# Attention sums kept transposed on four column tiles, with the softmax denominators sent through DRAM

## The chip, the cores and the metric

One Trainium2 chip, one of its cores. The metric is the device time of one execution in microseconds, the median of several runs. The time before is 291.59 us (three runs, 291.12 to 291.71).

## What is computed

A gated mix of two branches over one sequence of 2048 tokens with 512 features, all in bf16. Branch A is attention with a compressive memory: 32 heads of 16 features, four segments of 512 tokens, causal softmax attention inside a segment and a linear memory that is read before each segment's keys and values are added to it. Branch B is a gated MLP with 1792 hidden features.

```python
# branch A, for each segment s of 4 (L = 512 tokens), H = 32 heads, Dh = 16
logits = einsum('bhqd,bhkd->bhqk', qs, ks) * Dh**-0.5 + causal_mask
a_dot  = einsum('bhqk,bhkd->bhqd', softmax(logits), vs)
pq     = phi(qs)                        # t + 1 if t > 0 else exp(t)
a_mem  = (pq @ M) / (pq @ z + 1e-6)
o      = sigmoid(beta) * a_mem + (1 - sigmoid(beta)) * a_dot
M, z   = M + phi(ks).T @ vs, z + phi(ks).sum(over l)
a      = o @ wo
# branch B
b      = (gelu(x @ w_gate) * (x @ w_up)) @ w_down
# mix
g      = sigmoid((x * gate_w).sum(-1))
out    = g * a + (1 - g) * b
```

## The kernel before

**Chunks and groups.** Heads go in chunks `c` of eight (128 features), four chunks to a segment, 16 in all. The eight heads of a chunk are four pairs; `p` = 0 or 1 names the even or the odd head of each pair, and a chunk has two sides, p = 0 and p = 1. For each chunk, five groups A to E make the lower triangle of the logits: `group_qk` (L514) puts four heads on four row tiles of TensorE (32 rows each), one exp of 128x2048 on ScalarE turns the logits tile `lg` (four PSUM banks, one buffer) into `pT` (keys on partitions, queries along the free axis; five buffers), and GpSimd's `affine_select` (L543) zeroes what lies above the diagonal. There are 80 groups.

**Sums of values.** `pv` (L547) takes 128x128 blocks of `pT` as weights and 17 columns of V (16 features and a one) as the moving side, and so makes sums and denominators in rows of queries: 40 matmuls for a side. `finish` (L557) divides: a reciprocal of the denominators, a multiplication by one minus the head's gate, and a multiplication from PSUM into `o2`. The memory's share is `tm` (L507, VectorE, out of `mem_num`) and is added to `o2` (L804); a transposing DMA (L570) then makes `oT` with features on partitions, which `u_out` (L412) multiplies by `wo`. The memory's denominators come from `u_den` (L472).

**Other work, and the order.** K, Q, V, gate, up, down and out projections, the memory update `u_M`, and the masks are units in nine streams. A planner written into the kernel keeps modelled times of TensorE and ScalarE (`passed`, `act`), emits one group's logits when it believes that the exp before it has ended, and fills the time between with units: `fill_to` (L654) takes the unit with the smallest wanted group number plus a weight for VectorE's backlog. `clock` counts groups, `later(n, f)` puts a step n groups on, and `after` (L785) holds what follows each group. The result is one fixed order of instructions on each engine; engines run in order and meet by semaphores. Three PSUM banks (`gen`) serve all units, one serves `od`. All DMAs are issued by SyncE (SP).

**Buffers.** `xT` holds all four segments of x. `G` holds the gate activations, three buffers of 14 blocks of 512, so that gates of segment 3 wait for `down` of segment 0. `osb`, the output rows, has three buffers.

A second path (`general`) recomputes everything with row maxima if a bound on the logits fails; with these inputs it isn't run.

The lines that decide the order around the groups:

```python
goal = ready_at + max(0.0, slack) / (n + 1)
fill_to(t_pe[0] + 0.5 * (goal - t_pe[0]))
for f in pending:
    f()
pending.clear()
fill_to(goal)
t_pe[0] = max(t_pe[0], ready_at)
pending.append(lambda a=(s, c, g, mine, oT, state): after(*a))
```

Of the kernel before, what the change touches and what calls it, by code (L numbers as in the profile page):

```python
# [13 lines left out]
P = 128  # L14
D = 512
# [8 lines left out]
NG = 3  # L24
# [8 lines left out]
QK_T = 0.41  # L33
TURN = 0.15
# [10 lines left out]
def kernel(  # L45
# [29 lines left out]

    def const(shape, dtype, name):
        return cpool.tile(shape, dtype, name=name, tag=name)

    xT = const([P, FC, S], BF, "xT")
# [13 lines left out]
    og = const([P, H], F32, "og")  # L93
    Macc = const([P, NC8, 8, 17], F32, "Macc")
    Mn = [const([P, NC8, 128], BF, f"Mn{i}") for i in range(2)]
    Mz = [const([P, NC8, 8], BF, f"Mz{i}") for i in range(2)]
    rdm = [const([P, KT, H], F32, f"rdm{i}") for i in range(2)]
# [3 lines left out]
    G = [const([P, HS, L], BF, f"G{i}") for i in range(NG)]  # L101
# [4 lines left out]
    V = [const([P, KT, H, 18], BF, f"V{i}") for i in range(2)]  # L106
# [7 lines left out]

    def gen(name):
        return pgen.tile([P, 512], F32, name=name, tag="gen")

    def load_inputs():
        def cols(dst, src):
            nc.sync.dma_start(dst[:, :, :], src.rearrange("(fc p) n -> p fc n", p=P))  # L120

        def x_seg(s):
            nc.sync.dma_start_transpose(xT[:, :, s * L:(s + 1) * L], x2[s * L:(s + 1) * L, :])
# [11 lines left out]
        x_seg(3)  # L135
# [3 lines left out]

    x0 = G[1][:, 0:KT, :]  # L140
    zero = G[1][:, KT, :]

# [23 lines left out]
    def setup_consts():  # L166
# [9 lines left out]
        for i in range(2):  # L176
            nc.gpsimd.memset(V[i][:, :, :, 16:17], 1.0)
        nc.gpsimd.memset(Macc[:, :, :, :], 0.0)

    def setup_beta():  # L180
# [5 lines left out]
                                op0=ALU.mult, op1=ALU.add)  # L186

# [6 lines left out]
    def u_absmax_x(s):  # L194
        def f():
            for fc in range(FC):
                def g(fc=fc):
                    absmax(4 * (s - 1) + fc, xT[:, fc:fc + 1, s * L:(s + 1) * L])
                    passed(0.0, 0.6)
                later(1 + fc, g)  # L200
# [37 lines left out]
    def u_q(s, c):  # L238
        def f():
            T = gen("qT")  # L240
            for fc in range(FC):
                nc.tensor.matmul(T[:, :], lhsT=wq[:, fc, c * P:(c + 1) * P],  # L242
                                 rhs=xT[:, fc, s * L:(s + 1) * L],
# [9 lines left out]
    due = {}  # L253

    def later(n, f):
        due.setdefault(clock[0] + n, []).append(f)

    general_now = [False]
# [34 lines left out]
    def u_k(s, c):  # L293
        def f():
            T = gen("kT")
            for fc in range(FC):
                nc.tensor.matmul(T[:, :], lhsT=wk[:, fc, c * P:(c + 1) * P],  # L297
                                 rhs=xT[:, fc, s * L:(s + 1) * L],
# [16 lines left out]
    def u_v(s, kt):  # L315
        def f():
            T = gen("vT")
            for fc in range(FC):
                nc.tensor.matmul(T[:, :], lhsT=xT[:, fc, s * L + kt * P:s * L + (kt + 1) * P],  # L319
                                 rhs=wv[:, fc, :], start=(fc == 0), stop=(fc == FC - 1))  # L320
                if fc < FC - 1:
                    yield MM512
            nc.vector.tensor_copy(V[s % 2][:, kt, :, 0:16],
                                  T[:, :].rearrange("p (h d) -> p h d", h=H))
# [3 lines left out]
    def u_gate_logits(s):  # L328
        def f():
            T = gen("zT")  # L330
            for qt in range(KT):
                t = s * KT + qt
                for fc in range(FC):
                    nc.tensor.matmul(T[:, qt:qt + 1], lhsT=xT[:, fc, t * P:(t + 1) * P],
# [3 lines left out]
            if s < NSEG - 1:  # L338
                return 0.44
            g2 = gct[:, :, :].rearrange("p s q -> p (s q)")  # L340
            o2 = omg[:, :, :].rearrange("p s q -> p (s q)")
# [5 lines left out]
            def f_gate():  # L347
# [4 lines left out]
                done["gate"] = 1  # L352
# [6 lines left out]
    def u_gate(s, hs, direct):  # L359
        def f():  # L360
            T = gen("gT")
            for fc in range(FC):
                nc.tensor.matmul(T[:, :], lhsT=wga[:, fc, hs * P:(hs + 1) * P],  # L363
                                 rhs=xT[:, fc, s * L:(s + 1) * L],
# [3 lines left out]
            if direct:  # L368
                nc.scalar.activation(G[s % NG][:, hs, :], T[:, :], AF.Gelu_apprx_tanh)  # L369
            else:  # L370
                nc.vector.tensor_copy(G[s % NG][:, hs, :], T[:, :])  # L371
# [3 lines left out]
    def gelu(s):  # L375
        for h0 in range(0, HS, 7):
            g = G[s % NG][:, h0:h0 + 7, :]
            nc.scalar.activation(g, g, AF.Gelu_apprx_tanh)  # L378

    def u_up(s, hs):  # L380
        def f():
            T = gen("uT")
            for fc in range(FC):
                nc.tensor.matmul(T[:, :], lhsT=wup[:, fc, hs * P:(hs + 1) * P],  # L384
                                 rhs=xT[:, fc, s * L:(s + 1) * L],
# [3 lines left out]
            g = G[s % NG][:, hs, :]  # L389
# [6 lines left out]
    def u_down(s, qt):  # L396
        def f():
            T = gen("dT")
            for hs in range(HS):
                nc.tensor.matmul(T[:, :], lhsT=G[s % NG][:, hs, qt * P:(qt + 1) * P],  # L400
# [11 lines left out]
    def u_out(s, qt):  # L412
        def f():
# [7 lines left out]
            if s == NSEG - 1:  # L421

                osb = G[(s + 1) % NG][:, qt, :]
            else:
                osb = wk2.tile([P, D], BF, name="osb", tag="osb", bufs=3)[:, :]
# [8 lines left out]
    def u_M(s, half):  # L434
        def f():
            T = gen("MT")
            Tv = T[:, 0:272].rearrange("p (c h e) -> p c h e", c=2, h=8)
            for cc in range(2):
                c = 2 * half + cc
                for kt in range(KT):  # L440
                    nc.tensor.matmul(Tv[:, cc], lhsT=pk[:, kt, c * P:(c + 1) * P],  # L441
                                     rhs=V[s % 2][:, kt, 8 * c:8 * c + 8, 0:17],
# [8 lines left out]
    def u_mask(s):  # L451
        def half(h0):
            nc.vector.tensor_tensor(
# [557 lines left out]
```

## Time and profile before

| what | value |
|---|---|
| median of three runs | 291.59 us |
| profiled execution, its own time | 291.33 us |
| span of the profile | 289.4 us, granted TensorE clock 0.999 |
| PE busy (TensorE matmul) | 277.4 us, 96% |
| DVE busy (VectorE) | 215.5 us, 74% |
| ACT busy (ScalarE) | 200.7 us, 69% |
| POOL busy (GpSimd) | 82.7 us, 29% |
| first exp starts, last exp starts | 30.7 us, 273.1 us |
| the 16 output projections of the end | 282.1 to 285.6 us |
| DMA share | 70 to 100% in the first 35 us, below 50% behind that |

PE is TensorE's matmuls and PEld its weight loads, which overlap. The profile gives for each matmul a start and a modelled end that includes the pipeline's drain, so the cost of a matmul in a stream is the distance between starts, not its duration. A group line reads: line of the kernel, engine, operation, output tile <- input tiles, shapes, count, then busy time and mean nanoseconds of one, then the idle time of the engine before it and what ended that idle time.

### The profile page before, as it was taken

The page shows a single profiled execution, that of the slowest core. Times are in us where ns is not written, and L with a number is a line of the kernel's source. Part 1 is how long each engine was busy: PE and PEld are TensorE (multiplying, and loading weights), DVE is VectorE, ACT ScalarE, POOL GpSimd, SP SyncE. Part 2 cuts the span into 40 slices and gives each one's busy share as a digit, 9 for nine tenths or more (in the row PEclk, how much of TensorE's full clock was granted, in tenths as well). Part 3 has the DMA queues.
Part 4 walks back from the last instruction along what each step waited for, and adds up shares of the span by engine and source line. Part 5 has one row for each costly group of instructions (what it writes and reads, how often), then busy time and mean ns, then how long its engine had stood idle before and what let it go on. Part 6 is the DMA issues. An engine that isn't in the chain of part 4 may idle for free.

```text
span 289.4 us, 6869 instructions
## 1 busy us (share of the span) xinstructions
PE 277.4 (96%) x2915; PEld 137.7 (48%) x2965; DVE 215.5 (74%) x422; ACT 200.7 (69%) x125; POOL 82.7 (29%) x140
## 2 busy tenths in 40 slices
PE   7999999999999999999999999999999999999994
PEld 3444454555444454555445444445454544444451
DVE  1897589768777869977878968988768567775545
ACT  3246977678898776776898785767658968677700
POOL 4000224334204424333410424242423033342410
PEclk9999999999999999999999999999999999999999
DMA  7989941110000100410000001032101001000102
GB/s 221 325 223 229 328 58 20 36 20 2 20 0 2 20 20 18 94 20 20 18 20 18 2 2 36 3 75 36 39 0 39 2 0 20 18 20 22 39 18 77
DMA packets 29441, 15.82 MB, mean 55 GB/s; under 512 B 21984, under 2 KB 28384, under 8 KB 29408
## 3 DMA queue, kind: packets, MB, share of 16 engines
q1 hardware_dynamic: 29408, 15.35, 21.1%
q8 instruction: 24, 0.39, 0.6%
q14 instruction: 9, 0.07, 0.1%
HBM read 8.14 MB, written 2.10 MB: 35 GB/s over the span
## 4 chain that ended last, share of the span: by engine, by line
PE 56%; DVE 3%; issue 1%; DVEq 0%
PE dT L400 14%; PE uT L384 10%; PE od L553 7%; PE gT L363 6%; PE lg L526 6%; PE aT L417 4%; PE kT L297 2%; PE vT L319 2%; PE qT L242 2%; PE mn L503 1%; PE MT L441 1%; DVE ktb L302 0%; DVE G L371 0%; DVE pha L274 0%; DVE o L563 0%
## 5 line engine op out<-in xcount | busy, mean ns | idle before, releaser
L532 ACT ACTIVATE pT<-lg 128x2048 bf16<-128x2048 f32 x80 | 150.1, 1876 | 57.0 <-PE lg L526 45.7
L543 POOL TENSOR_SCALAR_AFFINE_SELECT pT<-pT 128x512 bf16<-128x512 bf16 x128 | 79.5, 639 | 192.7 <-ACT pT L532 192.7
L384 PE MATMUL uT<-xT,wup 128*128 128x512 bf16 x208 | 59.5, 379 | 1.3 <-issue 0.6
L363 PE MATMUL gT<-xT,wga 128*128 128x512 bf16 x211 | 57.0, 379 | 1.0 <-DVE G L371 0.4
L400 PE MATMUL dT<-wdn,G 128*128 128x512 bf16 x212 | 53.2, 379 | 1.1 <-issue 0.3
L553 PEld LDWEIGHTS <-pT 128*128 128x128 bf16 x1280 | 43.6, 96 | 17.7 <-issue 0.4
L553 PE MATMUL od<-V,pT 128*128 128x17 bf16 x1280 | 43.9, 170 | 0.1
L390 DVE TENSOR_TENSOR G<-uT,G 128x512 bf16<-128x512 f32 x56 | 38.3, 685 | 7.2 <-PE uT L384 6.8
L371 DVE CAST G<-gT 128x512 bf16<-128x512 f32 x42 | 28.8, 685 | 8.0 <-PE gT L363 7.7
L526 PE MATMUL lg<-QT,KT 32*128 32x384 bf16 (+3 forms) x512 | 31.7, 301 | 1.6 <-issue 1.5
L363 PEld LDWEIGHTS <-wga 128*128 128x128 bf16 x224 | 19.7, 97 | 22.8 <-issue 5.5
L400 PEld LDWEIGHTS <-G 128*128 128x128 bf16 x224 | 19.5, 97 | 22.2 <-issue 3.9
L384 PEld LDWEIGHTS <-wup 128*128 128x128 bf16 x224 | 19.2, 97 | 20.8 <-issue 5.0
L405 DVE TENSOR_SCALAR tB<-dT,omg 128x512 bf16<-128x512 f32 x16 | 12.0, 750 | 19.9 <-PE dT L400 19.8
L526 PEld LDWEIGHTS <-KT 32*128 32x128 bf16 x512 | 8.9, 92 | 29.9 <-issue 29.5
L378 ACT ACTIVATE G<-G 128x3584 bf16<-128x3584 bf16 x6 | 18.8, 3182 | 0.0
L559 DVE RECIPROCAL rden<-od 128x16 f32<-128x16 f32 x32 | 8.2, 256 | 13.4 <-PE od L553 13.2
L297 PE MATMUL kT<-xT,wk 128*128 128x512 bf16 x63 | 16.8, 380 | 0.3 <-DVE xT L162 0.2
L417 PE MATMUL aT<-wo,oT 128*128 128x512 bf16 x63 | 16.4, 379 | 0.5 <-DVE G L371 0.5
L242 PE MATMUL qT<-xT,wq 128*128 128x512 bf16 x57 | 16.2, 379 | 0.5 <-DVE QT L247 0.2
L319 PE MATMUL vT<-wv,xT 128*128 128x512 bf16 x64 | 16.4, 380 | 0.0
L369 ACT ACTIVATE G<-gT 128x512 bf16<-128x512 f32 x14 | 8.4, 597 | 9.5 <-PE gT L363 9.5
(84 smaller groups left out, 224.7 us busy)
## 6 DMA issues: line engine op xcount, KB each, us to landing
wga<-in_B_w_gate_dram SPq DMA_DIRECT2D x1, 1792.0 KB, 12.6
wup<-in_B_w_up_dram SPq DMA_DIRECT2D x1, 1792.0 KB, 9.1
wdn<-in_B_w_down_dram SPq DMA_DIRECT2D x1, 1792.0 KB, 9.1
out_dram<-osb SPq DMA_DIRECT2D x12, 128.0 KB, 1.7
G<-in_A_x_dram SPq DMA_DIRECT2D x1, 512.0 KB, 4.1
wk<-in_A_wk_dram SPq DMA_DIRECT2D x1, 512.0 KB, 5.0
wq<-in_A_wq_dram SPq DMA_DIRECT2D x1, 512.0 KB, 6.7
wv<-in_A_wv_dram SPq DMA_DIRECT2D x1, 512.0 KB, 8.7
```

Of the source, the lines that this page charges most:

```text
L297: nc.tensor.matmul(T[:, :], lhsT=wk[:, fc, c * P:(c + 1) * P], rhs=xT[:, fc, s * L:(s + 1) * L], start=(fc == 0), stop=(fc == FC - 1))
L319: nc.tensor.matmul(T[:, :], lhsT=xT[:, fc, s * L + kt * P:s * L + (kt + 1) * P], rhs=wv[:, fc, :], start=(fc == 0), stop=(fc == FC - 1))
L363: nc.tensor.matmul(T[:, :], lhsT=wga[:, fc, hs * P:(hs + 1) * P], rhs=xT[:, fc, s * L:(s + 1) * L], start=(fc == 0), stop=(fc == FC - 1))
L371: nc.vector.tensor_copy(G[s % NG][:, hs, :], T[:, :])
L384: nc.tensor.matmul(T[:, :], lhsT=wup[:, fc, hs * P:(hs + 1) * P], rhs=xT[:, fc, s * L:(s + 1) * L], start=(fc == 0), stop=(fc == FC - 1))
L390: nc.vector.tensor_tensor(out=g, in0=T[:, :], in1=g, op=ALU.mult)
L400: nc.tensor.matmul(T[:, :], lhsT=G[s % NG][:, hs, qt * P:(qt + 1) * P], rhs=wdn[:, hs, :], start=(hs == 0), stop=(hs == HS - 1))
L417: nc.tensor.matmul(T[:, :], lhsT=oT[:, fc, qt * P:(qt + 1) * P], rhs=wo[:, fc, :], start=(fc == 0), stop=(fc == FC - 1))
L526: nc.tensor.matmul(lg[:, j, off:off + n], lhsT=KTm[pp][32 * j:32 * j + 32, (NC8 * s + c) % NK, kt * P:(kt + 1) * P], rhs=QT[32 * j:32 * j ...
L532: nc.scalar.activation(pT[:, :, :], lg[:, :, :], AF.Exp, scale=DH ** -0.5)
L543: nc.gpsimd.affine_select(out=v, in_=v, pattern=pat, compare_op=ALU.is_ge, fill=0.0, base=0, channel_multiplier=-1)
L553: nc.tensor.matmul(od[:, qq, j, 0:17], lhsT=t[:, j, o:o + P], rhs=V[s % 2][:, kt, 8 * c + 2 * j + p, 0:17], start=(kt == 0), stop=(kt == qq))
```

## The change

Chunks other than the last two of the last segment no longer make rows of queries. `pv_side` takes V as weights (32 columns for a head: 16 features and 16 ones, in an order that depends on p) and blocks of `pT` as the moving side, on four column tiles, so that sums come out with features on partitions, and the denominators are repeated on the 16 partitions beside them. VectorE copies the bank to SBUF in f32 (`E0`, `E1`). One row of denominators for each head goes to DRAM, comes back folded over 128 partitions, is inverted and multiplied by the gate there, goes to DRAM again and comes back spread over each head's 16 partitions (`R`). Four DMAs bring the odd heads' sums from E1 into E0, and GpSimd multiplies E0 by R into `oT`. The memory part takes the same way with its own denominators (`u_den`, `mem_spread`, `mem_num`) and is added to `oT` on VectorE. The transposing DMAs of `oT` go away for these chunks.

To make room, `xT` keeps three segments (the fourth is loaded into the slot of the first during the loop), `G` becomes five blocks of seven, and `osb`, `o2` have one buffer. The planner gets a cost for `pv_side` and other conditions. Where code was only re-indexed it is left out.

```diff
-NG = 3
+XS = 3
+NG = 5
+PV_T = 0.75
+    ddr = ctx.enter_context(tc.tile_pool(name="ddr", bufs=2, space=bass.MemoryType.DRAM))
-    G = [const([P, HS, L], BF, f"G{i}") for i in range(NG)]
+    G = [const([P, 7, L], BF, f"G{i}") for i in range(NG)]
-    V = [const([P, KT, H, 18], BF, f"V{i}") for i in range(2)]
+    V = [const([P, KT, H // 2, 48], BF, f"V{i}") for i in range(2)]
...
-                osb = wk2.tile([P, D], BF, name="osb", tag="osb", bufs=3)[:, :]
+                osb = wk2.tile([P, D], BF, name="osb", tag="osb", bufs=1)[:, :]
...
+    def spread(R, dr, part):
+        a = dr[part:part + 8, :]
+        nc.sync.dma_start(R[:, :], bass.AP(a.tensor, a.offset, [[L, 8], [0, 16], [1, L]]))
+    def fold(dr, n):
+        a = dr[0:n, :]
+        return bass.AP(a.tensor, a.offset, [[4 * n, P], [1, 4 * n]])
...
     def u_den(s, pair):
...
+            for cc in range(2):
+                nc.tensor.matmul(T[32 * cc:32 * cc + 32, :],
+                                 lhsT=Mz[s % 2][:, 2 * pair + cc, :, :].rearrange("p h r -> p (h r)"),
+                                 rhs=pq[s % 2][:, 2 * pair + cc, :], start=True, stop=True,
+                                 tile_position=(0, 32 * cc))
+            wide = wk2.tile([P, L], F32, name="E1", tag="E1", bufs=1)
+            nc.vector.tensor_scalar_add(wide[0:64, :], T[0:64, :], 1e-6)
+            slim = wk2.tile([P, 64], F32, name="Cz", tag="Cz", bufs=1)
+            din, dout = (ddr.tile([16, L], F32, name=n, tag=n) for n in ("zin", "zout"))
+            def gather():
+                nc.sync.dma_start(din[:, :], wide[0:64:4, :])
+                nc.sync.dma_start(slim[:, :], fold(din, 16))
+            def invert():
+                nc.vector.reciprocal(slim[:, :], slim[:, :])
+                nc.vector.tensor_scalar(out=slim[:, :], in0=slim[:, :],
+                                        scalar1=gz[:, pair:pair + 1], scalar2=None, op0=ALU.mult)
+                nc.sync.dma_start(fold(dout, 16), slim[:, :])
...
+    def mem_spread(s, c):
...
+        R = wk2.tile([P, L], F32, name="Rm", tag="Rm", bufs=1)
+        spread(R, dout, 8 * (c % 2))
     def mem_num(s, c):
-        for qq in range(KT):
-            nc.tensor.matmul(T[:, qq * P:(qq + 1) * P],
-                             lhsT=pq[s % 2][:, c, qq * P:(qq + 1) * P], rhs=Mn[s % 2][:, c, :],
-                             start=True, stop=True)
+        nc.tensor.matmul(T[:, :], lhsT=Mn[s % 2][:, c, :], rhs=pq[s % 2][:, c, :],
+                         start=True, stop=True)
+        tm = wk2.tile([P, L], BF, name="tm", tag="tm")
+        nc.vector.tensor_tensor(out=tm[:, :], in0=T[:, :], in1=mem_R[c][:, :], op=ALU.mult)
...
+    def pv_side(s, c, p, blocks):
+        T = pod.tile([P, L], F32, name="odT", tag="od")
+        for kt in range(KT):
+            t, off = blocks[(p, kt)]
+            for j in range(4):
+                nc.tensor.matmul(T[32 * j:32 * j + 32, kt * P:L],
+                                 lhsT=V[s % 2][:, kt, 4 * c + j, 16 * p:16 * p + 32],
+                                 rhs=t[:, j, off:off + L - kt * P],
+                                 start=(kt == 0), stop=(kt == KT - 1), tile_position=(0, 32 * j))
...
+        nc.vector.tensor_copy(E[:, :], T[:, :])
+        def gather():
+            nc.sync.dma_start(din[p:8:2, :], E[16 * (1 - p):P:32, :])
+            if p == 1:
+                nc.sync.dma_start(slim[:, :], fold(din, 8))
+                for j in range(4):
+                    own = slice(32 * j + 16, 32 * j + 32)
+                    nc.sync.dma_start(E0[own, :], E[own, :])
...
+        later(1, gather)
+    def side_end(s, c, oT):
...
+        def invert():
+            nc.vector.reciprocal(slim[:, :], slim[:, :])
+            nc.vector.tensor_scalar(out=slim[:, :], in0=slim[:, :],
+                                    scalar1=oz[:, c:c + 1], scalar2=None, op0=ALU.mult)
+            R = wk2.tile([P, L], F32, name="R", tag="R", bufs=1)
+            nc.sync.dma_start(fold(dout, 8), slim[:, :])
+            spread(R, dout, 0)
+            def scale():
+                nc.gpsimd.tensor_tensor(out=oT[:, c, :], in0=E0[:, :], in1=R[:, :], op=ALU.mult)
+            later(2, scale)
+        def add():
+            if s > 0:
+                nc.vector.tensor_tensor(out=oT[:, c, :], in0=oT[:, c, :], in1=tms[c][:, :],
+                                        op=ALU.add)
+            done["tr", s] = count(("tr", s)) + 1
+        later(3, invert)
+        later(6, add)
...
+    us += [unit((0.0, 0.0, lambda: x_seg(NSEG - 1)), 20, None,
+                lambda: clock[0] >= 20 and count(("up", 0)) == HS)]
...
-                    lambda s=s: s < NG or count(("down", s - NG)) == KT) for hs in range(HS)]
+                    lambda b=2 * s + hs // 7: b < NG or count(("down", (b - NG) // 2)) == KT)
+               for hs in range(HS)]
...
+    def in_rows(s, c):
+        return s == NSEG - 1 and c >= NC8 - 2
     def after(s, c, g, blk, oT, st):
+        if g == "D" and s > 0:
+            room_for_bank()
+            mem_num(s, c)
+        if not in_rows(s, c):
+            return
...
+    def sides(s, c, g, blk, oT):
+        if g == "E" and not in_rows(s, c):
+            pv_side(s, c, 0, blk)
+            passed(PV_T, EVAC)
+            chunk_before.append((s, c, blk, oT))
+        if g == "B" and chunk_before:
+            s0, c0, blk0, oT0 = chunk_before.pop()
+            pv_side(s0, c0, 1, blk0)
+            side_end(s0, c0, oT0)
+            passed(PV_T, EVAC)
...
+                sides(s, c, g, mine, oT)
+                if g == "B" and s > 0:
+                    later(1, lambda s=s, c=c: mem_spread(s, c))
                 ready_at = t_act[0]
```

`sides` runs right behind a group's logits, before the filling; the memory's denominators may not start in groups A and B (`clock[0] % 5 not in (1, 2)`).

## The prediction

> **What bounds the kernel now.** I read the page first (busy shares, the chain that ended last), then the groups, then the PE timeline of one steady stretch, the start of the timeline, and the DMA landings.
>
> ```profile
> PE 277.4 (96%) x2915; PEld 137.7 (48%) x2965; DVE 215.5 (74%) x422; ACT 200.7 (69%) x125; POOL 82.7 (29%) x140
> ...
> PE 56%; DVE 3%; issue 1%; DVEq 0%
> PE dT L400 14%; PE uT L384 10%; PE od L553 7%; PE gT L363 6%; PE lg L526 6%; PE aT L417 4%; PE kT L297 2%; PE vT L319 2%; PE qT L242 2%; PE mn L503 1%; PE MT L441 1%; DVE ktb L302 0%; DVE G L371 0%; DVE pha L274 0%; DVE o L563 0%
> ```
>
> TensorE is busy 96% of the span and heads the chain; no other engine passes 74%. So time taken out of PE's queue is time gained, as long as nothing makes PE wait. The queue in a steady stretch:
>
> ```profile
> start us, us, engine line op out<-in xcount [idle before <-releaser]
> 116.31 0.85 PE L553 MATMUL od<-V,pT 128*128 128x17 bf16 x28
> 117.02 0.34 PE L480 MATMUL zd<-Mz,pq 128*128 128x8 bf16 x8
> 117.22 0.38 PE L363 MATMUL gT<-xT,wga 128*128 128x512 bf16 x1
> ...
> 119.48 0.81 PE L363 MATMUL gT<-xT,wga 128*128 128x512 bf16 x3
> 120.22 0.39 PE L526 MATMUL lg<-QT,KT 32*128 32x512 bf16 x4
> 120.55 0.39 PE L363 MATMUL gT<-xT,wga 128*128 128x512 bf16 x1
> 120.77 1.03 PE L319 MATMUL vT<-wv,xT 128*128 128x512 bf16 x4
> 121.63 1.05 PE L553 MATMUL od<-V,pT 128*128 128x17 bf16 x36
> 122.54 0.41 PE L441 MATMUL MT<-V,pk 128*128 128x136 bf16 x4
> ```
>
> What counts is the distance between starts (the second column includes the pipeline's end). A 128x512 matmul takes 0.22 (120.55 to 120.77; four vT take 0.86). The 28 and 36 small PV matmuls take 0.71 and 0.91: 25 ns each, although each streams only 17 columns. Eight denominators take 0.20. Four row-tiled logit matmuls leave after 0.33 rather than 0.22, and they enter late: three gT begun at 119.48 need 0.65, the logits start at 0.74. So each change of the array's tiling costs about 0.10.
>
> **The change on PE.** Old PV is 40 matmuls for a side (one head parity p of a chunk of 8 heads): 40 x 25 ns = 1.00 us. New, `pv_side` makes 16: for kt = 0 to 3, four with V (32 columns wide) as weights on four column tiles, streaming 512, 384, 256, 128 columns. If the four run together, 1280 columns are 1280/512 x 0.216 = 0.54. It comes right behind the logits, whose way out is paid already, so one change of tiling more: 0.64. A change from row tiles to column tiles is in no row; if it costs a way out and a way in, 0.74. I take the middle, 0.69. Do four run together?
>
> ```profile
> L151 PE MATMUL warm<-G x8: 393/408/421, 4.0 to 4.2; 128*32 128x256 bf16 x8
> ...
> 4.01 0.62 PE L151 MATMUL warm<-G 128*32 128x256 bf16 x8
> ...
> L147 PE MATMUL warm<-G x6: 607/634/634, 1.3 to 3.5; 128*128 128x512 bf16 x6
> ```
>
> Eight matmuls of 256 columns on four column tiles last 0.62, the last one 0.42 of that: the second four start 0.20 after the first. Six full-width ones of 512 start between 1.3 and 3.5, 0.43 apart, hence 0.21 for 256. Four tiles thus took the time of one, but at half the steady pace. At full pace nothing shows it; bounds for 512 columns are 0.216 (as one stream) and 0.40 (warm-up pace). I take 0.216: the logits' four row-tiled streams do run together at that pace.
>
> 28 of 32 sides change (the last two chunks of the last segment keep the old path): 28 x (1.00 - 0.69) = 8.7 us saved, between 7.3 and 10.1. `mem_num` goes from four 128-column matmuls to one of 512: 0.22 either way, nothing. `u_den` goes from eight small ones (0.20) to two of 512 on two column tiles with a way in and out, 0.42: 6 x 0.22 = 1.3 lost. `u_M` streams the same 136 columns. PE's sum: 7.4 saved.
>
> **Does ACT allow it?** The logits have a single buffer, so exp, logits, exp is a serial loop. Exp takes 1.88, and starts now come 2.7 apart:
>
> ```profile
> 123.41 1.88 ACT L532 ACTIVATE pT<-lg 128x2048 bf16<-128x2048 f32 x1 [0.81 <-POOL pT L543]
> 126.12 1.88 ACT L532 ACTIVATE pT<-lg 128x2048 bf16<-128x2048 f32 x1 [0.83 <-PE lg L526]
> 128.64 1.88 ACT L532 ACTIVATE pT<-lg 128x2048 bf16<-128x2048 f32 x1 [0.65 <-PE lg L526]
> ```
>
> The shortest idle time here is 0.65, a period of 2.53. 80 groups have 80 x 0.15 = 12 us of room; 7.4 fits.
>
> **DVE.** For a chunk, two `finish` go (2 x (0.256 + 0.322 + 0.425) = 2.0) and two copies of 128x512 f32 from PSUM come (0.69 each, as the cast L302; its output is bf16, the nearest row there is), with a reciprocal of 128x32 (0.35 as gh L184) and a small multiply (0.18): 1.9. The addition of the memory part stays 0.43. `u_den` grows by about 0.44 (0.69 instead of 0.21, same reciprocal), the masks split into four calls add 0.2 a call: +4 us over the run, inside 74 us of idle time. What matters is waiting in DVE's queue, since the evacuations of PE's three general PSUM banks stand behind it. A wait of up to 2 x 0.86 - 0.69 = 1.0 us is absorbed by the other two banks.
>
> **The DMA chain.** SP's rows to size it:
>
> ```profile
> out_dram<-osb SPq DMA_DIRECT2D x12, 128.0 KB, 1.7
> ...
> oT<-o SPq DMA_TRANSPOSE x15, 2.4
> ...
> 101.18 0.36 SPq L430 DMA_DIRECT2D out_dram<-osb  x1
> ```
>
> An issue holds SP 0.36, a landing takes 1.7 to 2.4. A chunk now puts ten DMAs on SP in place of one transpose (p = 0: one; p = 1: write, fold read, four pieces E1 to E0; inverse: write, spread; memory: spread), plus three for each pair's denominators: about 4.1 us of issue, and 4.3 of blocking while a read waits for its write to DRAM, of a chunk's 13.4 us. SP can carry it, but it becomes an ordered chain; the out stores, the pk transposes and the late `x_seg(3)` queue in the same line (one transpose issue is 1.2).
>
> From `invert` at group E: DVE start and work 1.0, write 0.36 + 1.7, spread 0.36 + 1.7 to 2.4: R is there 5 to 6 us later. GpSimd's scale is put behind the selects of B, two groups later (5.3), with exp's 1.88 and two selects of 0.64 before it: R is needed at about 8.4. Two to three us of margin. The scale itself is in no row: a select of 128x512 takes 0.64, a second input stream doubles that at most, so 0.64 to 1.3; I take 1.1. GpSimd, busy 29%, hides it; behind it stand the selects, and their reader `pv_side` comes a group or more later. The DVE addition is issued one group after the scale (with s > 0, ten chunks). The scale ends at 1.88 + 1.28 + 1.1 = 4.3 after B's exp started, and DVE gets to the addition at 2.9 to 3.9: it waits 0.4 to 1.4, of which 1.0 is absorbed. 0 to 4 us over ten chunks.
>
> Other new waits: `u_den` writes into E1 while the four pieces may still be read (six times, up to 2); `osb` has one buffer instead of three, and `out` of a segment becomes ready six groups later, so two can come close together, with 1.7 + 0.36 between them (three times). Of all of these I charge 1.5 us, from 0 to 6.
>
> On shared ports: L304 takes 340 ns at the least and 825 at the most here, which is about what waiting for one select of 0.64 would do. The Trainium skill, SBUF — State Buffer (the section on engine ports and DMA ports), says that DVE and GpSimd share a port pair held exclusively for a whole instruction when DVE has two SBUF inputs or a two-port mode. By it, each 1.1 us scale could hold up a DVE operation once, within the waits charged above.
>
> Gates in five blocks: the second half of segment 2 waits for all of down(0), that of segment 3 for down(1). GELU of the last segment runs at 222 to 230; behind it must come 14 up (12.1), 4 down (12.1), 4 out (3.5), 28 us of PE before 285.6. Ten us later would still fit, the other work moves ahead: no cost taken, 3 us if PE runs out of filling once. The third x slot takes `x_seg(3)` out of the opening, where PE is over 97% busy from 10 us on: nothing.
>
> Sum: the profiled execution took 291.33 (span 289.4, median 291.59). 291.33 - 8.7 + 1.3 + 1.5 = **285.4**. Its own range is 281 (side at 0.64, no waits, denominators at 0.20) to 289 (side 0.74, 4 us of waits).
>
> **Rivals.** A, slower: the DMA chain becomes DVE's bound. If R lands 2.4 instead of 1.7 at each step and the chain stands behind a denominator's write and fold read (another 2.8), R arrives 10 after E's exp, the scale ends at 11.1, and DVE, at the addition by 8.6, waits 2.5; 1.5 more than is absorbed, ten times: +15 on a saving of 7.4 less the 1.5 counted already, 297.4. It decides from an average wait of 1.7. For it: ten DMAs in a strict queue, each wait ahead of evacuations. Against it: 2 to 3 us of margin, 26% idle DVE. Chance 0.22.
>
> B, column tiles don't pay: waves stay at the warm-up's pace, 1.00 a side with a switch of 0.10 to 0.20, 0.15 x 28 = 4 lost and the denominators 0.6 instead of 0.2, 2.4 lost: 291.33 + 4.2 + 2.4 + 1.5 = 299. For it, the only column-tiled row has that pace; against it, all of PE had it then. Chance 0.06.
>
> C, they pay in part: a quarter of the way between the bounds, 0.27 for 512 columns: a side is 0.68 + 0.15 = 0.83, 4.8 saved, denominators 0.27 + 0.20 instead of 0.20, 1.6 lost: 291.33 - 4.8 + 1.6 + 1.5 = 289.6. Chance 0.13. The Trainium skill, TensorE: Matmul & The Clock Gate (Part 3, measured speedup), gives 2.38 times for three column tiles of 512 columns, 0.79 of the ideal; 0.216/0.79 is this 0.27. The warm-up row here shows no such loss at half pace.
>
> **Numbers.** Forecast 0.59, A 0.22, C 0.13, B 0.06. A measurement of this kernel tells 0.2%, 0.6 us, from no change. Faster: the forecast, C and the light end of A, less what falls within 0.6: 0.68; same 0.04; slower 0.28. Range 280.5 to 297.5: it holds the forecast, C and half of A.
>
> **What would show it.** Right: PV groups of 128x32 weights whose 16 matmuls leave after 0.64 to 0.74; exp starts 2.6 apart; PE still the chain. A: DVE rows of the addition with idle time released by POOL or a DMA, summed over 10 us, and PE under 95%. B and C: the distance from the first to the second wave of a side, 0.40 or 0.27 instead of 0.22. The prediction is wrong if PE idles on something not listed here, or if a side costs over 0.8.

## The result, and the profile after

| | before | after |
|---|---|---|
| median | 291.6 us | 327.5 us (321.6 to 328.6) |
| profiled execution, span | 291.3 us, 289.4 us | 321.6 us, 319.8 us |
| ratio after/before | | 1.108 (95% interval 1.100 to 1.117) |
| first to last matmul start | 283.8 us | 313.9 us |
| of it, PE idle | 4.3 us | 34.3 us |
| the rest, PE's work | 279.5 us | 279.6 us |

The change made the kernel 11% slower. The executions of the changed kernel differ from one another by up to 2%, and the ratio rests on the two fastest (321.6 and 324.6 us). PE idle is worked out here and below from the trace in one way: of every distance between two successive matmul starts over 0.45 us, what exceeds 0.216 us. PE's work is the remainder, so the two always add up to the time from first to last start.

The page of the changed kernel, its engine line and the shares of the chain that ended last:

```profile
PE 285.2 (89%) x2221; PEld 118.0 (37%) x2221; DVE 221.5 (69%) x406; ACT 200.8 (63%) x126; POOL 104.4 (33%) x157
...
PE 49%; DVE 16%; DMA 12%; issue 8%; ACT 6%; POOL 4%; SPq 4%; DVEq 0%; POOLq 0%; ACTq 0%
```

No engine but GpSimd is fuller than before (33% of the span, 29% before), and the chain, which was PE nearly alone, now runs through VectorE, DMAs, SP and GpSimd: the loss is waiting. The sums themselves do what was predicted. The PE timeline around one side (start, duration with drain, line, count):

```profile
102.13 0.40 PE L662 MATMUL lg<-QT,KT 32*128 32x384 bf16 x8
102.46 0.73 PE L594 MATMUL odT<-pT,V 128*32 128x512 bf16 x16
103.12 0.82 PE L269 MATMUL qT<-xT,wq 128*128 128x512 bf16 x3
```

Sixteen matmuls on four column tiles take 0.66 us from start to start, 1280 columns at full pace (0.54) and one change of tiling. What VectorE waited for, from its list of waits (total us, times, longest):

```profile
DVE E L605 <- PE odT L594: 14.5, 18, 3.0
DVE E L605 <- DMA zin<-E: 12.8, 3, 5.4
DVE oT L640 <- POOL oT L634: 10.9, 6, 3.6
...
DVE tm L582 <- DMA Rm<-zout: 5.8, 4, 3.5
...
DVE osb L458 <- DMA out_dram<-osb: 4.0, 1, 4.0
```

The last four lines make 33.5 us of waiting for DMAs and GpSimd that the kernel before did not have. How such a wait comes about is seen in SP's timeline of one stretch (start, time to the end of the row's last issue; the 4.75 us of the two stores hold about 4.0 in which SP stands for the second `osb`):

```profile
111.64 0.33 SPq L610 DMA_DIRECT2D C<-din  x1
112.01 2.48 SPq L613 DMA_DIRECT2D E<-E  x4
114.53 0.65 SPq L514 DMA_DIRECT2D Rm<-zout  x1
115.22 4.75 SPq L462 DMA_DIRECT2D out_dram<-osb  x2
120.01 6.15 SPq L342 DMA_TRANSPOSE pk<-phk  x4
126.26 0.52 SPq L630 DMA_DIRECT2D dout<-C  x1
127.93 0.66 SPq L514 DMA_DIRECT2D R<-dout  x1
128.65 0.54 SPq L540 DMA_DIRECT2D zin<-E  x1
131.63 0.32 SPq L541 DMA_DIRECT2D Cz<-zin  x1
```

and VectorE's in the same stretch (in brackets the idle time before the row, and what ended it):

```profile
118.85 0.75 DVE L458 SCALAR_TENSOR_TENSOR osb<-aT,gct,tB 128x512 bf16<-128x512 f32 x1 [4.02 <-DMA out_dram<-osb]
...
120.11 0.67 DVE L535 TENSOR_SCALAR E<-zd 64x512 f32<-64x512 f32 x1
...
131.70 0.69 DVE L605 COPY E<-odT 128x512 f32<-128x512 f32 x1 [4.71 <-DMA zin<-E]
```

The store of the one `osb` buffer stands behind four pieces and a spread: VectorE waits 4.0 us for the buffer. At 120.11 the memory's denominators are put into E1. They could leave at 120.8; SP takes them at 128.65, behind four transposes (6.15 us), a write and the read that waits for it. Until they have left, the next copy into E1 stands, and with it every evacuation behind it in VectorE's queue: 4.71 us. PE has its PSUM banks full and stops, and then runs at half pace (PE timeline of the changed kernel, then two rows of its table by stretch: us, busy time of PE, PEld, DVE, ACT and POOL, granted clock, DMA):

```profile
134.84 1.87 PE L395 MATMUL gT<-xT,wga 128*128 128x512 bf16 x4 [3.58 <-DVE tB L437]
```

```profile
120.00:130.00 10.00, 10.00 (x86) 3.60 (x83) 5.40 (x10) 5.63 (x3) 2.16 (x4) 0.83 0.52 82
130.00:140.00 10.00, 6.42 (x35) 2.39 (x32) 6.51 (x12) 3.75 (x2) 3.68 (x6) 0.83 0.15 40
```

Four such matmuls take 1.03 elsewhere (at 100.31, for one) and 1.87 there, starts 0.43 apart. The granted clock is 0.83 in these stretches and in 210 to 230 and 280 to 290.

### The profile page after: what moved, and what is told of

Its sections match the earlier page's. It is cut to its first block, busy times and chain, and to the rows that moved or that the text cites. A ratio compares the mean times of both kernels' runs of the same rounds, so it can differ in the third digit from the quotient of the medians.

```text
span 319.8 us, 5682 instructions
## 1 busy us (share of the span) xinstructions
PE 285.2 (89%) x2221; PEld 118.0 (37%) x2221; DVE 221.5 (69%) x406; ACT 200.8 (63%) x126; POOL 104.4 (33%) x157
## 4 chain that ended last, share of the span: by engine, by line
PE 49%; DVE 16%; DMA 12%; issue 8%; ACT 6%; POOL 4%; SPq 4%; DVEq 0%; POOLq 0%; ACTq 0%
PE gT L395 11%; PE dT L432 8%; PE uT L416 8%; PE lg L662 5%; ACT pT L668 4%; PE odT L594 3%; PE vT L349 3%; PE kT L327 3%; DMA din<-E 3%; DMA zin<-E 2%; PE qT L269 2%; DMA Rm<-zout 2%; SPq L613 2%; PE aT L449 2%; POOL oT L634 2%
## 5 line engine op out<-in xcount | busy, mean ns | idle before, releaser
L679 POOL TENSOR_SCALAR_AFFINE_SELECT pT<-pT 128x512 bf16<-128x512 bf16 x128 | 82.2, 660 | 198.7 <-ACT pT L668 196.3
L416 PE MATMUL uT<-xT,wup 128*128 128x512 bf16 x224 | 62.9, 388 | 0.9 <-DVE G L403 0.5
L432 PE MATMUL dT<-wdn,G 128*128 128x512 bf16 x224 | 54.3, 380 | 0.3 <-DVE G L403 0.3
L605 DVE COPY E<-odT 128x512 f32<-128x512 f32 x28 | 19.3, 691 | 27.8 <-PE odT L594 14.5
L395 PEld LDWEIGHTS <-wga 128*128 128x128 bf16 x224 | 20.9, 98 | 33.3 <-issue 12.5
L662 PEld LDWEIGHTS <-KT 32*128 32x128 bf16 x512 | 10.1, 92 | 35.0 <-issue 34.9
L594 PE MATMUL odT<-pT,V 128*32 128x512 bf16 (+1 forms) x448 | 21.4, 314 | 0.0
L269 PE MATMUL qT<-xT,wq 128*128 128x512 bf16 x64 | 18.3, 403 | 3.4 <-DVE tm L582 3.1
L349 PE MATMUL vT<-wv,xT 128*128 128x512 bf16 x64 | 17.7, 395 | 3.1 <-DVE osb L458 3.1
L437 DVE TENSOR_SCALAR tB<-dT,omg 128x512 bf16<-128x512 f32 x16 | 11.9, 746 | 10.7 <-PE dT L432 10.7
L634 POOL TENSOR_TENSOR oT<-E,R 128x512 bf16<-128x512 f32 x14 | 18.4, 1317 | 1.7 <-DMA din<-E 1.1
```

The lines of the kernel that those rows point to most:

```text
L349: nc.tensor.matmul(T[:, :], lhsT=xT[:, fc, xcols(s, kt * P, P)], rhs=wv[:, fc, :], start=(fc == 0), stop=(fc == FC - 1))
L432: nc.tensor.matmul(T[:, :], lhsT=gates(s, hs)[:, qt * P:(qt + 1) * P], rhs=wdn[:, hs, :], start=(hs == 0), stop=(hs == HS - 1))
L594: nc.tensor.matmul(T[32 * j:32 * j + 32, kt * P:L], lhsT=V[s % 2][:, kt, 4 * c + j, 16 * p:16 * p + 32], rhs=t[:, j, off:off + L - kt * P] ...
L634: nc.gpsimd.tensor_tensor(out=oT[:, c, :], in0=E0[:, :], in1=R[:, :], op=ALU.mult)
L662: nc.tensor.matmul(lg[:, j, off:off + n], lhsT=KTm[pp][32 * j:32 * j + 32, (NC8 * s + c) % NK, kt * P:(kt + 1) * P], rhs=QT[32 * j:32 * j ...
L679: nc.gpsimd.affine_select(out=v, in_=v, pattern=pat, compare_op=ALU.is_ge, fill=0.0, base=0, channel_multiplier=-1)
```

## The experiments

Each median stands with the ratio to the kernel before, taken in the same job on the same chip, and its interval. Two theories to start with: **theory 1**, VectorE's queue stands still on the DMA chain that goes through SP; **theory 2**, the new order and the smaller buffers make PE idle by themselves.

**e1: no DMA chain.**

```diff
-                nc.sync.dma_start(din[p:8:2, :], ...), fold, four E1 to E0
-            nc.sync.dma_start(fold(dout, 8), slim); spread(R, dout, 0)
+            R = Rc          # constant tile; the same for Rm, C, Cz
```

> The changed kernel without any of its DMAs for denominators and without the four pieces E1 to E0: scale and memory multiply by a constant tile, the small reciprocals run on constants; all other instructions and their order stay. Theory 1 (VectorE's queue stands still on the DMA chain through SP): PE's saving is left alone, 281 to 286 us, PE idle time under 6 us. Theory 2 (the new fixed order and the smaller buffers make PE idle): still above 305 us.

302.98 us, 1.038 (1.031 to 1.045). Two thirds of the loss goes (PE idle 22.4, work 274.4), a third stays: theory 1 alone is not enough. VectorE's list of waits in this run:

```profile
DVE E L607 <- PE odT L596: 17.9, 23, 3.0
DVE oT L635 <- POOL oT L629: 15.7, 9, 3.5
```

The addition waits for GpSimd's scale with no DMA in sight: the scale takes 1.3 us and stands behind the selects.

**e2: the buffers alone, in the kernel before; e6: with the last gate later.**

```diff
+XS = 3                      # x slots, the last segment loaded late
+NG = 5                      # blocks of seven; osb bufs=1
-           unit(u_gate_logits(NSEG - 1), 36, None, lambda: clock[0] >= 34),   # e6 alone,
+           unit(u_gate_logits(NSEG - 1), 48, None, lambda: clock[0] >= 48)    # behind u_bound
```

> The kernel before with the smaller buffers alone: gates in five blocks of seven, three x slots with the late load, osb with one buffer; old sums of values. Theory 1: 291 to 295 us, the single osb costs a few VectorE waits. Theory 2: a good part of the 30 us, above 300 us.

> The kernel before with the smaller buffers, as before, but the last segment's mixing gate is computed from group 48 on instead of 34, so that its exp on ScalarE no longer falls behind the GELU of segment 2. If that one collision (VectorE waits 7.8 us, PE idles 7.7 us and then runs at half rate for a while) is the loss of the buffers: 291 to 295 us. If the gate blocks or the single osb cost by themselves: 299 us or more.

e2: 303.51 us, 1.042 (1.034 to 1.049). e6: 292.64 us, 1.0035 (1.0020 to 1.0051). In e2 nearly all of it is one place, seen in ScalarE's timeline of e2, and in VectorE's:

```profile
148.55 6.27 ACT L386 ACTIVATE G<-G 128x3584 bf16<-128x3584 bf16 x2
154.84 1.28 ACT L351 ACT_TABLE_LOAD   x1
156.13 0.20 ACT L351 ACTIVATE gct<-gct 128x4 f32<-128x4 f32 x1
```

```profile
156.37 0.17 DVE L355 TENSOR_SCALAR gct<-gct 128x4 f32<-128x4 f32 x1 [7.84 <-ACT gct L351]
```

The last segment's mixing gate, moved because its x is loaded late, puts a 0.2 us exp behind two GELUs and a table load, and VectorE stands for it 7.84 us. Moved to group 48 it costs nothing to speak of, and gate blocks, x slots and the single `osb` together cost about 1 us. The changed kernel and e1 show no such wait; e4 and e5 ran into it (5.3 us each).

**e3 and e4: single waits mended.**

```diff
-            wide = wk2.tile([P, L], F32, name="E1", tag="E1", bufs=1)
+            wide = wk2.tile([P, L], F32, name="Ez", tag="Ez", bufs=1)
-        later(6, add)                       # e4 alone, with osb bufs=2 (shared with o2)
+        later(8, add)
```

> The changed kernel with a buffer of its own for the memory's denominators, which shared E1 (room from a second buffer of a 128-byte tile that is used once). Theory 1: the E1 copies no longer wait for the write of zin (12.8 us in three waits, which cost PE 6 to 8 us and half-rate clock behind them): 308 to 314 us. Theory 2: unchanged, 320 or more.

> As the last one, and two buffers for osb (shared with o2, which is used in the last segment only) and the addition of the memory part two groups later. Theory 1: the waits on the out store (4.0 us) and on GpSimd's scale (10.9 us) go too; what is left are the waits for Rm (5.8 us): 290 to 300 us. Theory 2: 315 or more.

e3: 325.54 us, 1.116 (1.109 to 1.124). e4: 324.54 us, 1.112 (1.104 to 1.120). Both misses. The waits named are gone or smaller, and others took their place: in e3 the E1 copies wait 2.9 us for zin in place of 12.8, but Cz waits 5.3 for it, tm waits 9.3 for Rm (5.8 before), the addition 15.0 (10.9 before). In e4 the waits for the out store and for GpSimd's scale are gone, tm waits 10.1, and the gate's collision comes in. The lateness stays, and whoever reads next pays it.

**e5: no chain, addition later.** As e1, with `later(8, add)` and two `osb`.

> As the run without the DMA chain, with the addition of the memory part two groups later and two buffers for osb. Theory 1a (of the 20 us that stayed without the chain, most are VectorE standing at the addition for GpSimd's scale, 15 us in eight waits): 286 to 293 us, no VectorE wait on GpSimd. Theory 2 (the new order and the gate blocks make PE idle by themselves): above 298 us.

303.59 us, 1.045 (1.039 to 1.051). A miss, but not a clean one: the waits on GpSimd are gone, PE idles 19.4 us all the same. Two groups later the addition falls on the group that also has the next chunk's inverse and the E0 copy, and the gate's exp falls behind the GELU.

**e7 and e8: half of the chain.** e7 leaves the memory's DMAs out, e8 the attention's.

> The changed kernel with the attention's DMA chain kept and the memory's left out (its denominators' write, fold, inverse, spread; the memory is multiplied by a constant tile). Theory 1 (SP's queue is the bound, the cost goes with what stands in it): the memory's chain holds SP for 1.9 us of issue and up to 1 us of blocking a chunk, less than a third: 310 to 318 us. A rival: the waits come from one chain only; then this is near 303 or stays at 320.

> The other half: the memory's DMA chain kept, the attention's left out (rows of denominators, fold, inverse, spread and the four pieces E1 to E0; scaled by a constant tile). Theory 1: two thirds of SP's load is gone: 304 to 311 us. The rival: the memory's chain alone makes the waits (zin, Rm), 315 us or more.

e7: 310.10 us, 1.067 (1.062 to 1.072). e8: 306.95 us, 1.055 (1.050 to 1.060). As theory 1 had it: taking out either half gives back 13 to 16 us, both together about 20, so neither chain alone is the culprit. One queue with both in it would do this. So would VectorE, which has to meet the landings of both in its own fixed order; these two runs don't tell the two apart.

**e9: no chain, three steps moved.** As e1, with two `osb`, the gate from group 48 on, and

```diff
+                ready_at = t_act[0]                  # moved up with them
+                for f in due.pop(clock[0], []):      # ahead of the side's sums, not behind
+                    f()
                 sides(s, c, g, mine, oT)
-        later(6, add)
+        later(7, add)
```

> Without the DMA chain, as before, and with three steps moved: the memory's addition one group later (not two, which put it behind the inverse and the next E0 copy), the last segment's gate from group 48 on (away from the GELU), a group's due steps ahead of its pv_side, so that VectorE does the small inverse and phi work while PE still runs the logits; osb with two buffers. Theory 1b (what stays without DMAs is VectorE standing at steps put at bad places in its fixed order): 284 to 291 us, the saving of the column tiles comes out. Theory 2 (the transposed sums or the new order cost more by themselves): 298 or more, as the last one.

292.41 us, 1.0024 (1.0002 to 1.0046): PE idle 12.2, work 271.8. It is a little above the 284 to 291 us that theory 1b asked for, and it tells two things. PE's work is 7.7 us less than before. And it doesn't show: PE idles 7.9 us more. The PE timeline of e9 at one of the places:

```profile
176.47 0.40 PE L657 MATMUL lg<-QT,KT 32*128 32x512 bf16 x4
176.88 0.81 PE L455 MATMUL aT<-wo,oT 128*128 128x512 bf16 x3
178.41 0.39 PE L455 MATMUL aT<-wo,oT 128*128 128x512 bf16 x1 [0.72 <-DVE oT L635]
```

**e10 and e11: SP's waits split off, pieces merged on GpSimd, one at a time.**

```diff
-                nc.sync.dma_start(slim[:, :], fold(din, 8))        # e10: one group later,
-            spread(R, dout, 0)                                     # both reads
+        later(2, gather2)
+            later(1, back)
-                    nc.sync.dma_start(E0[own, :], E[own, :])       # e11: four of them
+                nc.gpsimd.tensor_scalar(out=E0, in0=E0, scalar1=eo[:, 0:1], ...)
+                nc.gpsimd.tensor_scalar(out=E, in0=E, scalar1=eo[:, 1:2], ...)
+                nc.gpsimd.tensor_tensor(out=E0, in0=E0, in1=E, op=ALU.add)
```

> The changed kernel with each DMA that reads back from DRAM issued one group after the one that wrote, so that SP does not stand between the two; the same DMAs, the scale at the same group. If SP's standing between write and read (29 us for the attention's, 11 for the memory's) makes the lateness: 308 to 316 us. If it is the issue time of all the DMAs in one queue: 318 to 326 us.

> The changed kernel with the four DMAs E1 to E0 of a chunk replaced by three GpSimd operations (E0 and E1 times a mask, and their sum). SP loses 56 issues of 0.62 us, 35 us. If issue time in SP's queue is what makes the chain late: 308 to 316 us. If not: 320 or more, or slower, since GpSimd's operations stand before the selects.

e10: 325.50 us, 1.116 (1.112 to 1.120). e11: 332.68 us, 1.134 (1.128 to 1.140). SP's standing between write and read is not it by itself. The test isn't clean, though: with the read one group later, the four pieces stand ahead of it, and VectorE waits 6.1 us for C (1.0 in the changed kernel). e11 lies above the 308 to 316 us that issue time alone asked for, but it says little on SP: `u_den` shares E1 with the merge, and VectorE stood 10.7 us once for GpSimd to be done with it.

**e12 and e13: all mends, with the merge and with the pieces; e14: K's masked copies moved too.** Both have e10's split, e3's buffer, two `osb`, e9's three steps and one pk transpose a group; e12 has e11's merge; e14 is e13 with the two masked K copies (L334) on GpSimd.

> All mends with the whole computation: reads one group after the writes, the merge on GpSimd, the pk transposes one a group, a buffer of its own for the memory's denominators, two for osb, the gate from group 48 on, due steps ahead of pv_side, the addition one group later. Theory 1 (SP's queue and VectorE's fixed order are all of the loss): 286 to 298 us. Theory 2: 305 or more.

> All mends, but E1 to E0 by the four DMAs again instead of GpSimd's three operations, which cost 5 us where they stood alone. If SP, no longer standing between writes and reads and with its transposes spread, has room for 35 us of issues: 292 to 297 us. If SP's issue time still makes the chain late: 300 us or more.

> As the last one, and the two masked copies of each K chunk (0.36 us each, 32 in all, 11.6 us) go from VectorE to GpSimd, which has room. If VectorE's bursts are what takes PE's saving: 4 to 6 us below the last one, 287 to 293, about the kernel before or a little faster. If not: the same as the last one.

e12: 296.70 us, 1.017 (1.012 to 1.022). e13: 315.08 us, 1.083 (1.078 to 1.087). e14: 313.43 us, 1.073 (1.067 to 1.079). With the whole computation, e12 gives back about 26 of the 31.5 us (the ratio goes from 1.108 to 1.017). e14 is 1.7 us below e13, less than half of the 4 to 6 us that were asked for. The only difference in the code of e12 and e13 is how E1 gets into E0: 56 issues in SP's queue, 0.58 us each in the trace, 33 us, cost 18 us of time. e13's list of VectorE's waits has what is late again:

```profile
DVE C L634 <- DMA C<-din: 16.3, 8, 4.7
```

In e12 that wait is 5.0 us in three. SP's timelines of the same chunk show how it comes about, in e13 and then in e12:

```profile
106.60 2.50 SPq L614 DMA_DIRECT2D din<-E  x2
109.88 2.47 SPq L618 DMA_DIRECT2D E<-E  x4
112.39 0.65 SPq L517 DMA_DIRECT2D Rm<-zout  x1
113.14 0.40 SPq L621 DMA_DIRECT2D C<-din  x1
```

```profile
108.55 0.51 SPq L614 DMA_DIRECT2D din<-E  x1
109.10 0.61 SPq L517 DMA_DIRECT2D Rm<-zout  x1
110.29 0.32 SPq L623 DMA_DIRECT2D C<-din  x1
```

In both, the second write of denominators leaves at 108.6. In e13 the four pieces stand between it and the read-back, which leaves at 113.14 instead of 110.29, and VectorE's inverse waits for it:

```profile
116.44 0.35 DVE L634 RECIPROCAL C<-C 128x32 f32<-128x32 f32 x1 [1.39 <-DMA C<-din]
```

So the pieces' issue time costs by what stands behind it in SP's queue. SP is not full: between 35 and 270 us its issues take 98 of 235 us in e13, 69 in e12 and 96 in the changed kernel. There the pieces stand behind the read (112.01 after 111.64 above), and VectorE waits for C 1.0 us in all. Whether the pieces would still cost 18 us in e13 if they stood behind the read was not tried, nor was issuing a part of the DMAs from another engine than SP. So it is shown that the pieces cost 18 us at that place in SP's queue; that issue time in this queue was the bound of the changed kernel is argued, not shown.

**e15 and e16: is it VectorE's load that eats PE's saving?** K's masked copies on GpSimd, in e9's kernel and in the kernel before.

```diff
-                nc.vector.tensor_scalar(out=KTm[p][:, (NC8 * s + c) % NK, :], in0=ktb[:, c, :],
+                nc.gpsimd.tensor_scalar(out=KTm[p][:, (NC8 * s + c) % NK, :], in0=ktb[:, c, :],
...
-        return 4 * MM512, EVAC + 0.6, f
+        return 4 * MM512, EVAC, f            # the planner's cost of the unit
```

> The run without DMAs and with the three steps moved (292.4 us: no VectorE wait of note, 11 us of PE idle time against 3.4 before), with the masked K copies on GpSimd. Theory 3 (PE's saving of about 7 us is there and PE gives it back waiting for VectorE's backlog): 285 to 289 us. Against it: 291 or more.

> The kernel before with the masked K copies on GpSimd, as a control. PE bounds it with 3.4 us of idle time, so by theory 3 freeing VectorE gives at most that: 289 to 292 us. If it gains as much as the run without the chain, what the K copies bring has nothing to do with the change.

e15: 295.00 us, 1.010 (1.006 to 1.013). e16: 295.83 us, 1.015 (1.012 to 1.017). Inconclusive as a test: both got slower, and the order changed with the planner's costs. The group line of e16 shows what a copy takes on GpSimd (1571 ns, against 403 ns on VectorE before), and its PE waits show that PE then waits for the selects behind it, for 2.3 us:

```profile
L304 POOL TENSOR_SCALAR KT<-ktb,eo 128x512 bf16<-128x512 bf16 x32 | 49.8, 1571 | 4.3 <-DVE ktb L302 4.3
```

```profile
PE od L553 <- POOL pT L543: 2.3, 4, 0.8
```

**e17 and e18: the same question with work left out and no order changed.**

```diff
-            nc.vector.reciprocal(slim[:, :], slim[:, :])          # e17, in e9's kernel
-            nc.vector.tensor_scalar(out=slim[:, :], in0=slim[:, :], ...)
-        nc.vector.reciprocal(rden[:, :, :, :], od[:, :, :, 16:17])  # e18, in the kernel before
-        nc.vector.tensor_tensor(out=rden[:, :, :, 0], in0=rden[:, :, :, 0], ...)
```

> The run without DMAs and with three steps moved (292.4 us), in the same order on every engine, with the small inverses and their multiplications on VectorE left out (40 instructions, 14.1 us; their results go nowhere in that run). If VectorE's backlog is what makes PE give its saving back (theory 3): 285 to 289 us, PE idle 4 to 7 us in place of 11. If PE loses it otherwise: 291 or more.

> The control: the kernel before, in the same order, with the reciprocal and the small multiplication of each finish left out (64 instructions, 18.5 us of VectorE; it multiplies by a constant tile). PE had 3.4 us of idle time, so by theory 3 at most that is to be had: 289 to 291.5 us. If this gains as much as the other, VectorE's load is no cost of the change.

e17: 290.23 us, 0.9976 (0.9959 to 0.9993). e18: 289.86 us, 0.9954 (0.9939 to 0.9969). The medians of e9 and e17 are 2.2 us apart, but they come from two jobs. Each against the kernel before in its own job, 14.1 us less on VectorE take e9's kernel from 1.0024 to 0.9976, 1.4 us (PE's idle time goes from 12.2 to 10.6), and 18.5 us less give the control 1.4 us too. The gain is as large in the control, so these runs don't show VectorE's load to be a cost of the change. The PE waits that stay in e17:

```profile
PE uT L422 <- DVE tB L443: 1.7, 1, 1.7
...
PE zd L535 <- DVE Mz L507: 1.2, 1, 1.2
...
PE aT L455 <- DVE oT L628: 0.7, 1, 0.7
PE uT L422 <- DVE G L409: 0.7, 1, 0.7
PE mn L577 <- DVE osb L464: 0.6, 1, 0.6
```

Some of these are PE at a result that the fixed order makes VectorE produce just then (the mask for `u_den`, the sum in `oT` for `u_out`), the others are banks behind a burst. That moving them would give the rest was not tried.

## Why the prediction was wrong

The forecast was 285.4 us, faster, in a range to 297.5. The range, the sign and the likeliest case were wrong.

- **PE's sum was right.** Predicted 7.4 us saved; e9 and e17 have 271.8 us of work against 279.5, 7.7 saved. That it comes so near is in part luck: by the same count e1 saves 5.1 and e12 8.4, with the same matmuls in other orders. A side costs 0.66, between the 0.64 and 0.74 given. The column tiles stream together at full pace; rivals B and C are out (C's quarter of the way between the bounds is 0.26, not 0.27; nothing hangs on it). The Trainium skill's figure (TensorE: Matmul & The Clock Gate, Part 3), 2.38 times for three column tiles, does not hold for these streams: the second group of four starts 0.23 us behind the first, not 0.27.
- **The step that failed is the charge for waits,** 1.5 us with 6 as its upper end. It came to 30.0 us of PE idle time (34.3 against 4.3). Three terms in it were wrong. The issue time: I put 0.36 for every DMA, from the stores; it is 0.33 for a fold, 0.53 for a write of denominators, 0.58 for a piece and 0.64 for a spread, so a chunk holds SP 5.9 us and not 4.1 (2 x 0.53 + 0.33 + 4 x 0.58 + 0.35 + 2 x 0.64 + half of the three of a pair's denominators, 0.53, 0.33 and 0.36). The neighbours in the queue, named and priced at nothing: four pk transposes hold SP 6.15 us in one piece. And I followed one chain with an empty queue ahead of it; the margin of 2 to 3 us was for that alone.
- **Not all of the 30.0 us is the chain.** Without its DMAs (e1) PE's idle time falls by 11.9 us and its work by 5.2; with three steps moved and two `osb` as well (e9) by another 10.2 and 2.6. The second part is steps put at bad places in VectorE's fixed order. The prediction had one of them: VectorE waits 0.4 to 1.4 us at the addition, 0 to 4 us in all. In e1, with no DMA of the chain left, the addition waits 15.7 us in nine waits, 1.7 each.
- **Rival A was near the mechanism,** with a chance of 0.22, and its signs came: 10.9 us of waits at the addition, and PE at 89%. Its price was too low, since it looked at the addition alone; e3, e4, e7 and e8 show that any reader of the chain pays. Its sum has a slip too: the 7.4 holds no charge for waits, so there is no 1.5 to take off, and A is 298.9, beyond the range.
- **The part about the PSUM banks was right.** It put 1.0 us as what the two other banks absorb of a wait. At 118.85 VectorE's 4.02 became 3.13 of PE, at 131.70 its 4.71 became 3.58: 0.9 and 1.1 absorbed. The waits were longer than any that was priced.
- **A cost that the prediction had not at all** is the half pace behind some stops: PE's work is 279.6 us in the changed kernel and 271.8 in e9 with the same matmuls, 7.8 us. The granted clock, 0.83 in five stretches of 10 us, allows for up to 8.5 of it. But e1, with a clock of 0.997, has 274.4 us of work, so up to 2.6 of the 7.8 can come from the order. By the way they are counted, the three add up to the 30.1 us by which the time from first to last matmul grew: -7.7 + 30.0 + 7.8.
- **Gate blocks, x slots and osb** cost about 1 us in the kernel before (e6), about as put; in the changed kernel the one `osb` costs VectorE a wait of 4.0 us. The collision of the moved mixing gate with the GELU (e2) was not seen.
- **"ACT allows it"** held: the exps start 2.4 to 2.7 apart wherever nothing waits. But the claim behind it, that time out of PE's queue is time gained as long as nothing makes PE wait, was the whole question: even without the chain's DMAs (e9) PE idles 7.9 us more than before, and the gain is gone. Most of it is VectorE's: in the trace, waits of over 0.15 us for VectorE come to 9.0 us in e9 and 2.9 in the kernel before.

Open: how the 26 us that e12 gives back divide among its mends other than the merge, how much of the chain's lateness is SP's issue time and how much is SP and VectorE standing for each other, and whether another order would let PE's 7.7 us show. No version here beats the kernel before with the whole computation.

## What to carry to other kernels

Where one engine is 96% busy, a change that shortens it and adds a chain of dependent transfers trades work for order: size the queue that issues them with each form's own issue time, with all its neighbours in it, look at what each issue stands ahead of, and then ask which in-order engine stands at each landing. When waits move from one reader to the next as they are mended one by one, suspect what the readers share, and try mends together and take them out singly (e12 against e13). Test what a saving is worth first with the new chain replaced by constants (e1, e9): here it was worth nothing that shows.

## What the runs showed of the hardware

- PE runs at half pace behind some stops, and the length of a stop alone does not tell behind which. In the changed kernel stops of 3.13, 3.58 and 3.15 us (at 116.5, 131.3 and 214.9) are each followed by several us with starts 0.43 apart. Of two stops of 2.5 us, the one at 188.5 is not and the one at 277.4 is (PE's timeline, then the table by stretch, where the granted clock is 1.00 and 0.83):

```profile
191.07 0.39 PE L449 MATMUL aT<-wo,oT 128*128 128x512 bf16 x1 [2.54 <-DVE oT L640]
...
279.93 0.25 PE L689 MATMUL od<-V,pT 128*128 128x17 bf16 x4 [2.52 <-DVE E L605]
```

```profile
190.00:200.00 10.00, 8.13 (x62) 3.15 (x63) 9.31 (x20) 5.79 (x4) 3.36 (x6) 1.00 0.22 59
...
280.00:290.00 10.00, 10.00 (x92) 4.26 (x92) 7.39 (x17) 5.41 (x3) 2.37 (x4) 0.83 0.15 38
```

In e8 a stop of 1.97 us at 218.3 is followed by a clock of 0.83 (220 to 230 us), and in e5 one of 3.01 us at 153.0 is not (1.00 up to 170 us). The Trainium skill, TensorE: Matmul & The Clock Gate (Part 1), says that a window of about 3.4 us without work takes the clock to half. The trace does not bear this out as a length that a stop must have, since shorter stops are followed by the half clock; the measurement decides.

- GpSimd takes longer to multiply one tile by a value for each partition than two tiles by each other (e12, groups; mean ns of one; the sum of two tiles, L620, takes 1267):

```profile
L616 POOL TENSOR_SCALAR E<-E,eo 128x512 f32<-128x512 f32 x14 | 23.9, 1707 | 0.0
...
L647 POOL TENSOR_TENSOR oT<-E,R 128x512 bf16<-128x512 f32 x14 | 18.5, 1319 | 1.3 <-DMA R<-dout 1.3
```

- Four column tiles with 128 rows each stream four different moving tiles at the full pace of one: 0.66 us for 16 matmuls, against 1.00 for 40 small ones.
